# SyncE in program order, rows behind the sixth weight piece, and table constants on GpSimd

## The chip, the cores and the metric

One core of a Trainium2 chip. The metric is the device time of one execution in microseconds (us), the median over several runs. An execution has five engines that matter here: TensorE (PE; its weight loads are PEld), VectorE (DVE), ScalarE (ACT), GpSimd (POOL) and SyncE (SP), which only loads registers and issues DMAs.

## The reference

Clustered attention (2 batches, 8 heads, 768 positions, head size 64; a query sees the keys of its own cluster), then a dense layer on 1536 tokens, then a layer of 8 experts of which each token takes two. The last layer is what the change touches:

```python
def _moe2_ref(x, w_gate, w_noise, noise, w1, w2):
    logits = x @ w_gate
    noisy_logits = logits + np.log1p(np.exp(x @ w_noise)) * noise
    top2 = np.argpartition(-noisy_logits, 2, axis=1)[:, :2]
    ...
    for e in range(E):                      # E = 8, D = 512, F = 1024
        for k in range(2):
            mask = top2[:, k] == e
            h = np.maximum(x[mask] @ w1[e], 0.0)
            out[mask] += top2_w[mask, k, None] * (h @ w2[e])
```

## The kernel before, in words

**Stages.** Attention, the dense layer for batch 0 and for batch 1, a stage called `middle`, and the expert layer `moe2`; `rest` is a loop for overflowing tokens, which runs zero times on this input. Every token's row (512 numbers and 4 of routing) is scattered by POOL, by indirect DMA (`route_scatter`, L1043), into a DRAM table `xs` with a region for each expert. An expert reads its rows from there.

**Experts.** Experts 0 and 1 run in two halves of 240 rows, one per batch. The first halves, of batch 0, are computed in `middle` and at the start of `moe2`; meanwhile batch 1 is routed and scattered (six blocks, two scatters each). `gather_half(1)` (L1166, tile `Xh`) loads batch 1's rows of both experts; it has to wait for all of batch 1's scatters. Experts 2 to 7 are taken in an order found on the device (`ord`, `ordi`, ranked by their loads), with room for 432, 416, 408, 400, 392 and 384 rows.

**An expert's weights** come in eight pieces of 512 KB, in the order 0, 4, 1, 5, 2, 6, 3, 7 (`ORDER`): pieces 0 to 3 are columns of w1 (L1117), 4 to 7 rows of w2 (L1119). A piece lands in one of three staging buffers (`stg`); ACT rounds each half of it (L1126, "split" below) and DVE or POOL takes the remainder (L1130). Two sets of weight tiles (`wA` with `wg`, `wB` with `wx`) alternate between experts, so a piece's tiles come free when the expert before last has read them. An expert's rows (L1158, tile `X`) go into one buffer, which comes free when PE has transposed the rows before (L1229).

**In an expert** (`expert`, L1380 on) PE goes through eight blocks `fb`: first product (L1325), then ACT makes `hh` (L1333) and DVE `hl` (L1334), then the second product (L1348, or L1378 for experts 2 to 6). Results are weighted into `Y` by DVE (L1362) and scattered to the output by POOL (L1363); for all but a token's first expert `Y` starts from the rows gathered out of the output (L1210).

**What sets the order.** Each engine runs its instructions in one fixed order. Inside `manual_schedule(engines=...)` the named engines keep the order in which the program emits them; everything else, and where an ordered engine's instructions fall among those emitted outside, is placed by a planner from its own estimate of times. In attention all engines are ordered by hand, in `middle` all but POOL (table `WIN`); in `moe2` none is (but PE in the last expert's tail), SP included. `moe2` emits, on SP: `gather_half(1)`; then for each expert 2 to 7 a register load of its number (L1433), its eight pieces, its rows (`load`, L1432). An expert's `load` is emitted one turn ahead of its work.

**The rounds' table.** `route_end` (called near the end of `middle`, due time `re`) runs on DVE: it clips the counts, ranks the experts (`rank`) and writes the table for `rest` (`table`, L1083 on), with constants that don't depend on data: memsets of `caps`, `cap`, `tb`, `mx`, and columns made of `ie`. One of the six routing copies that precede the scatters (L1041) comes behind it in DVE's order. `consts` (L622) makes other constants at step 1 of attention.

Of the kernel before, what the change touches and what calls it, by code (L numbers as in the profile page):

```python
# [613 lines left out]
class Moe:  # L614
# [38 lines left out]

    def init_piece(self, i):
# [395 lines left out]
    def route_end(self):  # L1050
        v, end = self.nc.vector, self.rtot[:, NB, 0:2]
# [3 lines left out]
        self.rank(self.rtot[:, NB, :])  # L1055
        self.table(self.rtot[:, NB, :])

    def rank(self, total):

        c, v, n = self.const, self.nc.vector, E - 2  # L1060
        key, pos = c.tile([128, n], F32, name="key"), c.tile([128, n], F32, name="rpl")
        big = self.rtile("big", n, n)
        self.ord, self.cap = c.tile([128, n], F32, name="ord"), c.tile([128, E], F32, name="cap")
        self.ordi = c.tile([128, n], I32, name="ordi")
        v.scalar_tensor_tensor(key, total[:, 2:], float(E), self.ie[:, 2:], op0=OP.mult, op1=OP.subtract)
        row = lambda a: a[:, None, :].to_broadcast([128, n, n])
        col = lambda a: a.rearrange("p (n o) -> p n o", o=1).to_broadcast([128, n, n])
        v.tensor_tensor(big, row(key), col(key), op=OP.is_gt)
        v.tensor_reduce(pos.rearrange("p (n o) -> p n o", o=1), big, axis=AX.X, op=OP.add)
        v.tensor_tensor(big, row(pos), col(self.ie[:, :n]), op=OP.is_equal)  # L1070
        at = self.rtile("at", n, n)
        v.tensor_tensor(at, big, row(self.ie[:, 2:]), op=OP.mult)
        v.tensor_reduce(self.ord.rearrange("p (n o) -> p n o", o=1), at, axis=AX.X, op=OP.add)
        v.tensor_copy(self.ordi, self.ord)
        caps = c.tile([128, n], F32, name="caps")
        for r, (cp, ck) in enumerate(CAPS):
            v.memset(caps[:, r:r + 1], float(cp * ck))
        v.tensor_tensor(at, big, col(caps), op=OP.mult)
        v.memset(self.cap[:, :2], float(CAP))
        v.tensor_reduce(self.cap[:, 2:].rearrange("p (n o) -> p n o", o=1), at.rearrange("p r n -> p n r"),  # L1080
                        axis=AX.X, op=OP.add)

    def table(self, total):  # L1083
        nc, v = self.nc, self.nc.vector
        tb = self.const.tile([128, ROUNDS, E, 4], F32, name="tb")
        v.memset(tb, 0.0)
        for r in range(1, ROUNDS):
            o = BASE + CMIN + (r - 1) * CAP
            v.tensor_scalar_add(tb[:, r, :, 0], total, float(-o))
            v.tensor_scalar(tb[:, r, :, 1], self.ie, float(REG), float(o), op0=OP.mult, op1=OP.add)  # L1090
            v.tensor_copy(tb[:, r, :, 2], self.ie)
        v.tensor_scalar_add(tb[:, 1, :, 3], self.cap, float(-CMIN))
        nc.sync.dma_start(self.tab.rearrange("(o r) n -> o (r n)", o=1), tb[0:1].rearrange("p r e n -> p (r e n)"))
        mx = self.const.tile([128, 1 + ROUNDS], F32, name="mx")
        left = self.const.tile([128, E], F32, name="left")
# [3 lines left out]
        v.memset(mx[:, 1:2], 1.0)  # L1099
        for r in range(1, ROUNDS):  # L1100
# [469 lines left out]
```

## Time and profile before

| | us |
|---|---|
| median of 3 runs | 939.82 (936.96 to 941.28) |
| the profiled execution, its own time | 941.51 |
| its span, first to last instruction | 939.6 |

The span is what the rows below are read from; the 1.9 us around it are start and end. Times in rows are us from the span's start. A timeline row gives start, length, engine, line, operation, written tile and read tiles, how many were merged, and in square brackets the idle time before it and what ended it. SPq and POOLq are the queues of instructions that issue or wait.

### The profile page before, as it was taken

To read this page: it belongs to the slowest core of one execution; us is meant where nothing else is said; L and a number is where in the kernel's file an instruction comes from. 1 tells how busy PE (TensorE), PEld (TensorE's weight loads), DVE (VectorE), ACT (ScalarE), POOL (GpSimd) and SP (SyncE) were. 2 spreads that over 40 slices of the span, in tenths; PEclk is the share of its full clock that TensorE was granted. 3 is DMA by queue.
4 is the path that set the end of the run, shared out by engine and by line. 5 is a ranking of instruction groups with operands and counts; after the bars stand their busy time and mean duration, and the time that the engine had idled before them with its cause. 6 is when DMAs were issued, how large, how long until landed. Compare 5 with 4: busy or idle time off the path is not lost. (4 is left out here: it accounts for less than half of the span.)

```text
span 939.6 us, 14934 instructions
## 1 busy us (share of the span) xinstructions
PE 887.8 (94%) x5277; PEld 812.0 (86%) x5277; DVE 592.7 (63%) x1190; ACT 489.6 (52%) x1021; POOL 374.8 (40%) x398
## 2 busy tenths in 40 slices
PE   6999999999898999999999999899999899999993
PEld 4898989899887888888998979888889799999992
DVE  3889898998884667675447643836564445555231
ACT  2788888888794556554445433414444243432210
POOL 3134443454455988880000601562341334342121
PEclk8999999999898999999999999899999899999997
DMA  8756675677331344311111331274774737552120
GB/s 212 192 145 184 165 202 137 177 186 206 110 127 33 111 135 119 118 42 61 44 28 32 144 88 46 90 243 121 242 208 117 182 109 210 171 178 68 33 66 35
DMA packets 77532, 120.14 MB, mean 128 GB/s; under 512 B 9858, under 2 KB 55939, under 8 KB 76941
## 3 DMA queue, kind: packets, MB, share of 16 engines
q1 hardware_dynamic: 69997, 100.98, 37.5%
q0 software_dynamic: 7456, 18.16, 6.1%
q8 instruction: 43, 0.70, 0.3%
q14 instruction: 36, 0.29, 0.1%
HBM read 72.85 MB, written 23.76 MB: 103 GB/s over the span
## 5 line engine op out<-in xcount | busy, mean ns | idle before, releaser
L434 DVE TENSOR_TENSOR PTl<-ps_pt,PTh 128x384 fp32r<-128x384 f32 x192 | 98.8, 549 | 11.5 <-ACT PTh L429 10.4
L429 ACT ACTIVATE PTh<-ps_pt 128x384 fp32r<-128x384 f32 x192 | 87.9, 497 | 29.1 <-PE ps_pt L419 28.0
L402 DVE TENSOR_REDUCE nm<-ps_s 128x1 f32<-128x768 f32 x96 | 91.2, 950 | 15.1 <-PE ps_s L397 14.8
L419 PE MATMUL ps_pt<-ident,P 128*128 128x128 f32 x576 | 88.2, 277 | 3.8 <-DVE PTl L434 3.5
L410 ACT ACTIVATE P<-ps_s,nm 128x768 f32<-128x768 f32 x96 | 87.3, 910 | 4.9 <-DVE nm L402 4.9
L1333 ACT ACTIVATE hh<-bank 128x240 fp32r<-128x240 f32 (+6 forms) x80 | 35.2, 446 | 90.7 <-PE bank L1325 84.7
L1325 PE MATMUL bank<-xT,wB 128*128 128x240 f32 (+3 forms) x480 | 82.1, 319 | 0.0
L419 PEld LDWEIGHTS ps_pt<-ident,P 128*128 128x128 f32 x576 | 68.4, 141 | 13.8 <-DVE PTl L434 10.8
L1325 PEld LDWEIGHTS bank<-xT,wB 128*128 128x128 f32 x480 | 76.7, 189 | 2.5 <-DVE hl L1334 0.3
L1130 POOL TENSOR_TENSOR wA<-stg,wA 128x512 fp32r<-128x512 f32 x16 | 20.7, 1296 | 139.1 <-DVE wol L714 66.7
L822 PE MATMUL bank<-woh,gh 128*128 128x512 f32 x192 | 76.2, 397 | 0.0
L822 PE MATMUL bank<-wol,gh 128*128 128x512 f32 x192 | 75.0, 391 | 0.0
L1334 DVE SCALAR_TENSOR_TENSOR hl<-bank,hh 128x240 fp32r<-128x240 f32 (+6 forms) x80 | 40.2, 505 | 49.0 <-ACT hh L1333 48.2
L396 PE MATMUL ps_s<-k,q 128*128 128x384 f32 x192 | 70.7, 368 | 0.4 <-ACT P L410 0.2
L822 PE MATMUL bank<-woh,gl 128*128 128x512 f32 x192 | 70.7, 391 | 0.0
L397 PE MATMUL ps_s<-k,q 80*128 80x384 f32 x192 | 66.3, 346 | 2.6 <-DMA q<-ohT 2.6
L1363 POOL DMA_INDIRECT out_dram<-Y,idx x31 | 33.2, 1071 | 77.3 <-DVE Y L1362 68.5
L1126 ACT ACTIVATE wA<-stg 128x512 fp32r<-128x512 f32 x52 | 32.5, 632 | 43.5 <-DMA stg<-in_moe_w_dram 15.6
L454 PE MATMUL ps_o<-PTl,vs 128*128 128x256 f32 x288 | 54.0, 296 | 0.0
L454 PE MATMUL ps_o<-PTh,vs 128*128 128x256 f32 x288 | 53.7, 295 | 0.3 <-ACT T L461 0.2
L1325 PE MATMUL bank<-xT,wA 128*128 128x240 f32 (+3 forms) x300 | 53.2, 328 | 0.0
L1325 PEld LDWEIGHTS bank<-xT,wA 128*128 128x128 f32 x300 | 49.6, 197 | 1.3
(311 smaller groups left out, 2322.6 us busy)
## 6 DMA issues: line engine op xcount, KB each, us to landing
stg<-in_moe_w_dram SPq DMA_DIRECT2D x64, 512.0 KB
q<-ABq SPq DMA_DIRECT2D x48, 192.0 KB
k<-ABk SPq DMA_DIRECT2D x48, 192.0 KB
si<-in_moe_w_in_dram SPq DMA_DIRECT2D x14, 512.0 KB
so<-in_moe_w_out_dram SPq DMA_DIRECT2D x14, 512.0 KB
xs<-zrow SPq DMA_DIRECT2D x24, 217.7 KB
ld<-in_k_dram SPq DMA_DIRECT2D x8, 384.0 KB
ld<-in_q_dram SPq DMA_DIRECT2D x8, 384.0 KB
```

What stands on the lines that cost most here:

```text
L396: self.nc.tensor.matmul(o, self.g("S1", u, "q")[:, h, qs], self.g("S1", u, "k")[:, h, ks], start=True, stop=False)
L397: self.nc.tensor.matmul(o, self.g("S2", u, "q")[:80, h, qs], self.g("S2", u, "k")[:80, h, ks], start=False, stop=True)
L402: self.nc.vector.tensor_reduce(nm, self.g("s", j)[:, :, :384], axis=AX.XY, op=OP.max, negate=True)
L410: self.nc.scalar.activation(P, self.t.pop(("s", j))[:, :, :384], AF.Exp, bias=self.t.pop(("nm", j)), scale=1.0, accum_out=self.g("sums", u ...
L419: self.nc.tensor.transpose(ps[:, k, :], P[:, k * 128:(k + 1) * 128], self.ident)
L429: self.nc.scalar.activation(self.pt_at(j, g, 0), self.g("pt", j, g), AF.Copy)
L434: self.nc.vector.tensor_sub(self.pt_at(j, g, 1), self.t.pop(("pt", j, g)), f(self.pt_at(j, g, 0)))
L454: self.nc.tensor.matmul(self.g("O", u, qp)[:, h, :], vs[:, h, 2 * i + half].rearrange("p a d -> p (a d)"), PTx[:, kc, :], start=(c == 1 an ...
L822: nc.tensor.matmul(acc[j], g[:, sl], w, start=(fb == 0 and n == 0), stop=(fb == FB1 - 1 and n == 2))
L1325: self.nc.tensor.matmul(ps, w[:, kb, :], xT[:, kb, x], start=(kb == 0 and i == 0), stop=(kb == KB - 1 and i == 2))
L1333: self.nc.scalar.activation(hh, ps, AF.Relu)
L1334: self.nc.vector.scalar_tensor_tensor(hl, ps, 0.0, f(hh), op0=OP.max, op1=OP.subtract)
```

## The change

SP is ordered by hand in `moe2` too. `load` issues an expert's rows behind its sixth weight piece instead of behind the eighth. In `route_end`, `rank` and `table` are merged; the clipping of the first two counts comes after the ranking; the parts that don't depend on data are made by POOL in `consts`; three instructions over a row each become one over three rows; the unused first row of the table is dropped. On DVE `route_end` has 18 instructions instead of 37; on POOL `consts` has 18 more.

```diff
     def consts(self):
...
+        g, n, r = nc.gpsimd, E - 2, ROUNDS - 1
+        self.caps, self.cap = c.tile([128, n], F32, name="caps"), c.tile([128, E], F32, name="cap")
+        for i, (cp, ck) in enumerate(CAPS):
+            g.memset(self.caps[:, i:i + 1], float(cp * ck))
+        g.memset(self.cap[:, :2], float(CAP))
+        self.tb, self.offs = c.tile([128, r, E, 4], F32, name="tb"), c.tile([128, r, E], F32, name="offs")
+        g.memset(self.tb, 0.0)
+        for i in range(r):
+            o = BASE + CMIN + i * CAP
+            g.memset(self.offs[:, i], float(o))
+            g.tensor_scalar(self.tb[:, i, :, 1], self.ie, float(REG), float(o), op0=OP.mult, op1=OP.add)
+            g.tensor_copy(self.tb[:, i, :, 2], self.ie)
+        self.mx = c.tile([128, 1 + ROUNDS], F32, name="mx")
+        g.memset(self.mx[:, 1:2], 1.0)
...
     def route_end(self):
...
+        v.tensor_tensor(self.tb[:, :, :, 0], total[:, None, :].to_broadcast([128, ROUNDS - 1, E]), self.offs,
+                        op=OP.subtract)
+        v.tensor_scalar_add(self.tb[:, 0, :, 3], self.cap, float(-CMIN))
...
+        v.tensor_tensor(mx[:, 2:], mx[:, 0:1].to_broadcast([128, ROUNDS - 1]), self.offs[:, :, 0], op=OP.is_gt)
...
-    def weights(self, e, par):
+    def weights(self, e, par, late=lambda: None):
         we = [w[bass.ds(e, 1)].rearrange("o k n -> (o k) n") for w in (self.w1, self.w2)]
         W = [None] * 8
-        for s in ORDER:
+        for n, s in enumerate(ORDER):
             W[s] = self.weights_part(e, par, s, we)
+            if n == 5:
+                late()
         return [x for p in W for x in p]
...
         def load(e):
             i = self.nc.values_load(self.ordi[0:1, e - 2:e - 1], engines=(mybir.EngineType.SP,), min_val=2, max_val=E - 1)
-            n["W"] = self.weights(i, e % 2)
-            n["X"] = self.gather(i, *CAPS[e - 2])
+            n["W"] = self.weights(i, e % 2, lambda: n.__setitem__("X", self.gather(i, *CAPS[e - 2])))
...
-    moe.moe2(s["W"], W1, *s["A"][1][1:])
+    with tc.manual_schedule(engines={mybir.EngineType.SP}):
+        moe.moe2(s["W"], W1, *s["A"][1][1:])
     moe.rest()
```

## Rows read from the trace of the kernel before

**Rows 1.** The page, busy time of each engine.

```profile
PE 887.8 (94%) x5277; PEld 812.0 (86%) x5277; DVE 592.7 (63%) x1190; ACT 489.6 (52%) x1021; POOL 374.8 (40%) x398
```

**Rows 2.** Timeline of PE, in the expert layer; brackets: idle before.

```profile
635.34 0.66 PE L1229 MATMUL bank<-ident,Xh 120*128 120x120 f32 x2 [2.88 <-DMA Xh<-xs]
...
642.85 1.19 PE L1348 MATMUL bank<-wA,hh 128*120 128x512 f32 x4
...
676.23 0.44 PE L1229 MATMUL bank<-ident,X 108*128 108x108 f32 x3
...
692.76 0.55 PE L1229 MATMUL bank<-ident,X 104*128 104x104 f32 x4 [0.90 <-DMA X<-xs]
...
742.14 3.14 PE L1378 MATMUL bank<-hh,wB 128*128 128x416 f32 x8 [3.92 <-ACT hh L1333]
```

**Rows 3.** Stretches: length, busy PE, PEld, DVE, ACT, POOL, PEclk, DMA share, GB/s.

```profile
635.10:638.50 3.40, 3.16 (x10) 2.54 (x11) 1.86 (x9) 0.74 (x2) 1.07 (x1) 0.50 0.76 189
...
740.90:747.80 6.90, 5.66 (x17) 5.30 (x18) 5.61 (x12) 3.48 (x7) 2.46 (x2) 0.51 0.48 160
```

**Rows 4.** Timeline of SP, 600 to 632 us.

```profile
615.19 0.40 SPq L1117 DMA_DIRECT2D stg<-in_moe_w_dram  x1
...
631.03 0.81 SPq L1166 DMA_DIRECT2D Xh<-xs  x2
```

**Rows 5.** Timeline of POOL, 620 to 636 us.

```profile
621.35 1.29 POOL L1130 TENSOR_TENSOR wB<-stg,wB 128x512 fp32r<-128x512 f32 x1
...
625.32 0.97 POOL L1043 DMA_INDIRECT xs<-R,rridx  x1 [0.30 <-issue]
...
635.12 1.07 POOL L1210 DMA_INDIRECT Y<-out_dram,idx  x1 [0.30 <-issue]
```

**Rows 6.** Line L1043 (batch 1's 12 scatters): issue to landing.

```profile
DMA to landing us min/median/max: 3.0/3.9/6.2
```

**Rows 7.** Waits of SP, 590 to 660 us: us in total, times, longest.

```profile
SPq L1166 <- DMA out_dram<-Y,idx: 5.8, 1, 5.8
```

**Rows 8.** Timeline of DVE: expert 1's first half put into Y.

```profile
639.08 1.41 DVE L1362 SCALAR_TENSOR_TENSOR Y<-bank,m,Y 120x512 f32<-120x512 f32 x2 [1.41 <-PE bank L1348]
```

**Rows 9.** Timeline of SP around the rows of experts 3 and 4.

```profile
684.60 0.34 SPq L1158 DMA_DIRECT2D X<-xs  x1
...
713.47 0.62 SPq L1119 DMA_DIRECT2D stg<-in_moe_w_dram  x1
727.04 0.29 SPq L1158 DMA_DIRECT2D X<-xs  x1
727.59 0.37 SPq L1117 DMA_DIRECT2D stg<-in_moe_w_dram  x1
```

**Rows 10.** Waits of SP, whole span: us in total, times, longest.

```profile
SPq L1158 <- PE bank L1229: 30.1, 3, 12.8
```

**Rows 11.** Timeline of ACT behind the rows of experts 4 and 5.

```profile
732.05 0.52 ACT L1333 ACTIVATE hh<-bank 128x416 fp32r<-128x416 f32 x1 [3.83 <-PE bank L1325]
740.53 1.15 ACT L1126 ACTIVATE wB<-stg 128x512 fp32r<-128x512 f32 x2 [7.96 <-DMA stg<-in_moe_w_dram]
...
778.22 0.51 ACT L1333 ACTIVATE hh<-bank 128x408 fp32r<-128x408 f32 x1 [2.78 <-PE bank L1325]
782.06 1.15 ACT L1126 ACTIVATE wg<-stg 128x512 fp32r<-128x512 f32 x2 [3.33 <-DMA stg<-in_moe_w_dram]
```

**Rows 12.** Timeline of DVE in `route_end`: first constants, and the copy behind it.

```profile
613.80 0.10 DVE L1077 MEMSET caps<- 128x1 f32 x6
...
614.73 0.25 DVE L1091 COPY tb<-ie 128x8 f32<-128x8 f32 x1
...
616.50 0.16 DVE L1041 COPY R<-rmeta 128x4 f32<-128x4 f32 x1
```

**Rows 13.** Timeline of POOL in attention: the last constant and what follows it.

```profile
14.03 0.13 POOL L637 IOTA re<- 128x8 f32 x1
41.22 1.01 POOL L341 TENSOR_TENSOR sc<-eq,rev 128x384 f32<-128x384 f32 x1 [27.06 <-DVE eq L335]
```

More of the change, by code (lines that the diff above doesn't have):

```diff
@@ L1050, in route_end @@
     def route_end(self):
-        v, end = self.nc.vector, self.rtot[:, NB, 0:2]
+        nc, c, v, n = self.nc, self.const, self.nc.vector, E - 2
+        total, end = self.rtot[:, NB, :], self.rtot[:, NB, 0:2]
+        row = lambda a: a[:, None, :].to_broadcast([128, n, n])
+        col = lambda a: a.rearrange("p (n o) -> p n o", o=1).to_broadcast([128, n, n])
+        key, pos = self.rtile("key", n), self.rtile("rpl", n)
+        big, at = self.rtile("big", n, n), self.rtile("at", n, n)
+        self.ord, self.ordi = c.tile([128, n], F32, name="ord"), c.tile([128, n], I32, name="ordi")
+        v.scalar_tensor_tensor(key, total[:, 2:], float(E), self.ie[:, 2:], op0=OP.mult, op1=OP.subtract)
+        v.tensor_tensor(big, row(key), col(key), op=OP.is_gt)
+        v.tensor_reduce(pos.rearrange("p (n o) -> p n o", o=1), big, axis=AX.X, op=OP.add)
+        v.tensor_tensor(big, row(pos), col(self.ie[:, :n]), op=OP.is_equal)
+        v.tensor_tensor(at, big, row(self.ie[:, 2:]), op=OP.mult)
+        v.tensor_reduce(self.ord.rearrange("p (n o) -> p n o", o=1), at, axis=AX.X, op=OP.add)
+        v.tensor_copy(self.ordi, self.ord)
+        v.tensor_tensor(at, big, col(self.caps), op=OP.mult)
+        v.tensor_reduce(self.cap[:, 2:].rearrange("p (n o) -> p n o", o=1), at.rearrange("p r n -> p n r"),
+                        axis=AX.X, op=OP.add)
         over = self.rtile("over", 2)
@@ L1054, in route_end @@
         v.scalar_tensor_tensor(end, over, float(MAIN), self.over[:, 0], op0=OP.add, op1=OP.add)
[L1055 to L1095, printed above, removed]
+        v.tensor_tensor(self.tb[:, :, :, 0], total[:, None, :].to_broadcast([128, ROUNDS - 1, E]), self.offs,
+                        op=OP.subtract)
@@ L1096, in table @@
+        v.tensor_scalar_add(self.tb[:, 0, :, 3], self.cap, float(-CMIN))
+        nc.sync.dma_start(self.tab.rearrange("(o r) n -> o (r n)", o=1),
+                          self.tb[0:1].rearrange("p r e n -> p (r e n)"))
+        left, mx = self.rtile("left", E), self.mx
         v.scalar_tensor_tensor(left, self.cap, float(BASE), total, op0=OP.add, op1=OP.is_lt)
@@ L1098, in table @@
         v.tensor_reduce(mx[:, 0:1], left, axis=AX.X, op=OP.max)
-        v.memset(mx[:, 1:2], 1.0)
-        for r in range(1, ROUNDS):
-            v.tensor_single_scalar(mx[:, r + 1:r + 2], mx[:, 0:1], float(BASE + CMIN + (r - 1) * CAP), op=OP.is_gt)
+        v.tensor_tensor(mx[:, 2:], mx[:, 0:1].to_broadcast([128, ROUNDS - 1]), self.offs[:, :, 0], op=OP.is_gt)
         self.nr = self.const.tile([128, 1], I32, name="nr")
@@ L1187, in gather_rest @@
         t = self.cs.tile([CP, 4], F32, tag="t", name="t")
-        nc.sync.dma_start(t, self.tab[bass.ds(r * E + e, 1)].to_broadcast([CP, 4]))
+        nc.sync.dma_start(t, self.tab[bass.ds((r - 1) * E + e, 1)].to_broadcast([CP, 4]))
         sl = self.cs.tile([CP, CK, 4], F32, tag="sl", name="sl")
@@ L1473 @@
     xs = dram.tile([E * REG, ROW], F32, name="xs")
-    tab = dram.tile([ROUNDS * E, 4], F32, name="tab")
+    tab = dram.tile([(ROUNDS - 1) * E, 4], F32, name="tab")
     ident = const.tile([128, 128], F32, name="ident")
```

## The prediction

> **What bounds the kernel now.** I read the page's busy times first. TensorE is busy 887.8 us, 94% of the span of 939.6 us [rows 1], so 51.8 us are all that can be won without taking work from it, and an edit counts only where PE stands still or runs at its low clock. The next view is PE's timeline through the expert layer, where three pauses fall in the part that the change reorders [rows 2]: 2.88 us at 632.5, until the second half's rows of experts 0 and 1 (`Xh`) have landed; 0.90 us at 691.9, until expert 3's rows (`X`) have landed; 3.92 us at 738.2, until ScalarE has made an `hh`. Behind the first and the third the stretches show a granted clock of 0.50 for 3.4 us and 0.51 for 6.9 us, which is the 1.2 GHz level instead of 2.4 [rows 3]. PE was busy 3.16 and 5.66 us there, so at the full level it would have needed about half: 1.6 and 2.8 us more are lost to the clock. The three pauses are thus worth 4.5, 0.9 and 6.7 us. The constants and the route's end run on VectorE and GpSimd, and neither appears in these three brackets.
>
> **Part 1: SP in the program's order.** In the trace of before SP issues three weight pieces of expert 2, the first at 615.19, and only then `Xh` at 631.03 [rows 4]. In program order `Xh` comes first. It can't leave before batch 1's scatters have landed. POOL issues the last at 625.32 [rows 5]; the twelve take 3.0 to 6.2 us to land, median 3.9 [rows 6]. The 5.8 us wait ahead of `Xh` is put down to an output scatter [rows 7], but the first of the last pair (1.3 us ahead of 625.32), at the maximum of 6.2, lands at 630.2 too, and the 6.2 fall where two of the three pieces move. Without these pieces I take 3.3, between the least and the median: 625.3 + 3.3 = 628.6, so `Xh` leaves 2.4 us earlier. From issue to PE's use it took 635.34 − 631.03 = 4.3 us; then PE would wait 0.45 instead of 2.88 us. So short a wait should spare the low clock, 1.6 us. That makes −4.0. What is late next: the second product of expert 0's second half (642.85 now, [rows 2]) needs the two banks which DVE empties into `Y` at 639.08 and, merged in one row, about 0.7 us later [rows 8]; that in turn needs output rows whose gather POOL issues at 635.12 [rows 5]. Emptied at 640.5 at the latest, the banks allow 2.4 us; with the gathers about 1 us earlier, as the scatters ahead of them lose the same traffic, 3.4. I take **−3.4**, bounds −4.5 (pause and clock gone) and 0 (the last scatter lands at its 6.2 whatever else moves). The three pieces leave some 15 us later, right behind `Xh`. Their tiles are free only when expert 0 has read them, from about 642 on, and at 4.3 us behind `Xh` they are there by then: 0. If that cover were gone, the splits of ACT ahead of the next `hh` would be late by what is missing.
>
> What waits in SP's order: `Xh` now stands ahead of everything of expert 2, including the register load of its number, and the six loads of numbers stay each with its expert. A load of a register is under 1 us and each comes before a transfer that waits for a buffer anyway: 0.
>
> **Part 2: rows behind the sixth piece.** Expert 3's rows leave SP at 684.60, right behind the last piece [rows 9], though their buffer is free when PE has transposed expert 2's rows, at 676.7 [rows 2]. Two pieces earlier they leave by 677, land some 7 us earlier, and the pause at 691.9 goes: **−0.9**, bounds −0.9 and 0. For expert 2 the same is worth nothing, as PE has no pause at its transposes.
>
> From expert 4 on it is otherwise. SP reaches the rows at 714.1 and can't issue them until 727.04 [rows 9]: the buffer is held by expert 3's transposes. Three such waits sum to 30.1 us, the longest 12.8 [rows 10]. The rows leave at the same moment after the change, but the two pieces behind them, 3 and 7, now wait as well: SP reaches the rows already behind the sixth piece, so that some 7 to 12 us more of SP's time are a wait, and the experts' last two pieces leave behind the rows instead of ahead of them. Behind expert 4's rows today follow three pieces of expert 5; then it will be two of expert 4 and one of expert 5. As many bytes leave at the same moment. None of these pieces is due soon: expert 4's first `hh`, at 778.22, comes 51 us after its rows have left [rows 9, 11]. So the moved issues (two pieces and one transfer of rows, six times) cost PE nothing by themselves. What decides is where the planner puts their splits in ACT's order. Today one such split stalls ACT for 7.96 us at 732.6, because the first piece behind the rows takes from 727.59 to 740.53, and the `hh` behind it makes PE's pause of 3.92 [rows 9, 11]. I take this pause as staying: **0**, bounds −6.7 (pause and clock gone) and +17.0 (below).
>
> The Trainium skill ("DMA: Bandwidth & Descriptors", section "Why a DMA increments its semaphore by 16 and not by 1") says that a transfer from SP's queue runs on the largest number of DMA engines up to 16 that divides its rows: 102 partitions (expert 4) get six, 128 sixteen. By it the transfer of 102 rows is the slowest and holds up most what follows on its engines; the 12.9 us of the piece behind it agree.
>
> **Part 3: the route's end on DVE.** 19 of 37 instructions go. Six memsets take 0.10 merged, three table columns 0.25 [rows 12]; at 0.06 to 0.08 us each the 19 are 1.1 to 1.5 us, and the routing copy behind them at 616.50 comes that much earlier. The scatter that reads it starts only at 624.0, after ten others and two tensor operations on POOL, the first at 621.35 [rows 5, 12], so the gain lies beside POOL's work: **0**. Bounds: 0 and −2.6, if the planner, with the copy ready sooner, puts the last two scatters ahead of those two operations; that gain is inside the −4.5 above. The moved clipping has the same cost in a new place.
>
> **Part 4: 18 instructions on POOL in attention.** They follow the last constant at 14.03; then POOL idles 27.06 us [rows 13]. The nearest row, the 128x8 iota, takes 0.13, so they need 2.4 us: hidden eleven times over. The price can only be DVE, held up while POOL works on the same memory: at most the 2.4 us, at least 0. I take **+0.2**, near the small end, since the operands are 8 to 96 numbers a row.
>
> **Sum.** −3.4 − 0.9 + 0 + 0 + 0.2 = −4.1 against the profiled execution's 941.51 (span 939.6 and 1.9 around it): 937.4. That execution lies 1.7 us above the median of 939.82, so on the median's scale **935.7**. About 0.5%, 4.7 us, is what a measurement of this kernel can tell from no change, so this forecast lies just inside the band.
>
> **The rivals.**
>
> *A, the pause at 738 goes too.* SP's forced order changes the planner's times, and with other pieces behind expert 4's rows ACT's order there is made anew. If `hh` comes ahead of the late split, 3.92 + 2.8 us are saved: 935.7 − 6.7 = 929.0. For it: PE needs `hh` at 738 and ACT is idle from 732.6. Against it: the planner put a split there once, and the same bytes are as late.
>
> *B, the late splits come ahead of the first `hh` (slower).* The tiles of an expert's pieces 3 and 7 are free when the rows leave, while those of the next expert's first pieces come free only when its first product is read. So the planner may set pieces 3 and 7 earlier in ACT's order than today's splits. Behind expert 4's rows the first `hh`, at 732.05 now, would wait for the landing at 740.53 and two halves of 0.6: PE pauses 9.1 instead of 3.9 us, +5.2. Behind expert 5's the `hh` at 778.22 would wait for the piece that was there at 782.06: to 783.2, +5.0. For experts 6 and 7 no row shows the case; I take half, 2.6 each. With 1.6 of low clock: +17.0, so 953. It is slower than before as soon as a quarter of it (4.2 us) comes true, that is, one expert's rows; half of it gives 944. Against it: ACT waited 3.33 us for a piece behind expert 5's rows without any pause of PE [rows 11].
>
> By the rule of the Trainium skill in “DMA: Bandwidth & Descriptors” named above, the harm would be largest behind expert 4's rows and least behind expert 7's; it would shift B's prices between the experts, not their start.
>
> *C, `Xh` leaves no earlier.* If its release is the output scatter that the row names (issued behind the last scatter of rows), or the scatters land as late without the pieces, only 0.9 is won: 939.82 − 0.7 = 939.1.
>
> **How the numbers follow.** Forecast (sum holds, pause at 738 stays, between 933 and 938): 0.37. A: 0.25. B: 0.21. C: 0.17. Faster by over 0.5% (below 935.1): all of A and about half of the forecast, as its bounds (−4.5, 0 for `Xh`) lie on both sides: 0.44. Slower (above 944.5): most of B: 0.18. Within: 0.38. The range takes in the forecast, C, A with 2 us more, and B to its half: 927 to 947.
>
> **What would show it.** SP's timeline: `Xh` ahead of all pieces of expert 2, at about 628.6; the landing of the last scatters near 3.3 us. PE's timeline: no `Xh` pause over 1 us and clock 1.00 behind it; no pause on `X`. POOL: a block of 18 instructions at 14 to 17 us with an idle stretch of over 20 us behind it. ACT's timeline at the rows of experts 4 to 7: which comes first, a split waiting for `stg` or `hh`. I am wrong if `Xh` still leaves after 630.5, or if PE's waits for `hh` in the expert layer, 3.92 us in the largest now, sum to over 10 us.

## The result, and the profile after

The changed kernel takes **949.41 us** (median of 16 runs, 940.67 to 955.60) against 939.52 for the kernel before (16 runs, 936.61 to 941.61): a ratio of **1.0099, 95% interval 1.0080 to 1.0118**. It is slower by 1%, where 935.7 was forecast, and lies above the range. Two of the changed kernel's runs, 955.29 and 955.60, count as slow and are not in the ratio. Its profiled execution took 949.89 us, span 948.1.

The page's busy times of the kernel after show no more work on PE than [rows 1]:

```profile
PE 885.6 (93%) x5277; PEld 808.1 (85%) x5277; DVE 596.2 (63%) x1171; ACT 490.1 (52%) x1021; POOL 377.4 (40%) x416
```

So PE stands still more. Timeline of PE after, the four longest pauses of the expert layer (compare [rows 2]):

```profile
629.94 0.63 PE L1226 MATMUL bank<-ident,Xh 120*128 120x120 f32 x4 [1.67 <-DMA Xh<-xs]
...
686.54 1.02 PE L1226 MATMUL bank<-ident,X 104*128 104x104 f32 x5 [4.80 <-DMA X<-xs]
...
745.57 1.75 PE L1375 MATMUL bank<-hh,wB 128*128 128x416 f32 x4 [4.41 <-ACT hh L1330]
...
802.98 1.39 PE L1375 MATMUL bank<-hl,wA 128*128 128x408 f32 x3 [2.68 <-DVE hl L1331]
```

The pause on `Xh` shrank from 2.88 to 1.67 us. The one on expert 3's rows, which was to vanish, grew from 0.90 to 4.80; the one for `hh` stayed, and one for `hl` is new. Stretches of both kernels, before first: from PE's first transposes of `Xh` to expert 2's first product, then the stages of experts 2, 3 and 4, each from its first product to the next (columns as in [rows 3]):

```profile
635.34:685.59 50.25, 50.04 (x322) 43.77 (x323) 31.58 (x72) 24.47 (x55) 15.16 (x13) 0.97 0.58 180
685.59:727.26 41.67, 40.77 (x215) 38.40 (x214) 21.73 (x36) 17.71 (x35) 13.43 (x11) 1.00 0.57 164
727.26:773.50 46.24, 42.32 (x225) 41.08 (x224) 20.25 (x36) 14.45 (x30) 14.18 (x12) 0.93 0.54 145
773.50:813.33 39.83, 39.08 (x225) 38.31 (x225) 21.00 (x39) 16.40 (x32) 14.54 (x12) 1.00 0.57 168
```

and after, with two rows more for the stretches behind the pauses at 686.54 and 745.57 (granted clock 0.53 and 0.51, the 1.2 GHz level):

```profile
629.94:690.31 60.37, 52.50 (x336) 45.34 (x336) 32.89 (x76) 26.05 (x57) 18.64 (x15) 0.97 0.65 198
690.31:730.11 39.80, 39.80 (x207) 37.84 (x206) 19.87 (x32) 14.88 (x29) 10.86 (x9) 1.00 0.41 111
730.11:777.18 47.07, 42.66 (x226) 41.36 (x224) 22.04 (x37) 15.02 (x31) 14.31 (x12) 0.93 0.53 143
777.18:821.54 44.36, 40.79 (x226) 39.83 (x224) 23.16 (x38) 15.72 (x31) 14.55 (x12) 0.96 0.51 150
686.40:690.00 3.60, 3.46 (x13) 2.92 (x14) 1.10 (x2) 1.41 (x3) 1.27 (x1) 0.53 0.32 115
744.80:751.70 6.90, 6.13 (x18) 5.88 (x19) 6.15 (x8) 4.06 (x8) 5.38 (x5) 0.51 0.54 166
```

I call the first two stretches together **S1** (from `Xh` to expert 3) and the other two **S2** (experts 3 and 4). S1 went from 91.9 to 100.2 us, S2 from 86.1 to 91.4. Behind S2 nothing changed (813.33 to PE's last matmul at 924.29 before, 821.54 to 932.65 after: 111.0 and 111.1).

These 13.6 us are more than the 8.5 between the spans, because S1 also starts 5.4 us earlier. Only a part of that is the change's. Timeline of PE before, at the last matmuls of the routing (`rrM`) and at a first product of the second halves, 244 matmuls later in both orders:

```profile
600.97 0.22 PE L993 MATMUL bank<-rrM,tri 128*128 128x48 bf16 x1 [2.38 <-DVE rrM L943]
...
644.56 1.51 PE L1325 MATMUL bank<-xT,wg 128*128 128x240 f32 x12
```

and after, with a later pause in between:

```profile
597.80 0.20 PE L1008 MATMUL bank<-rrM,tri 128*128 128x48 bf16 x1 [2.37 <-DVE rrM L958]
...
638.55 0.71 PE L1322 MATMUL bank<-xT,wg 128*128 128x240 f32 x4 [1.02 <-DVE xT L1229]
...
641.19 1.50 PE L1322 MATMUL bank<-xT,wg 128*128 128x240 f32 x12
```

At `rrM` this execution stood 3.2 us ahead of the one before; a second profile of the same changed program (after_2 below) stood 2.0 us behind it (602.99). So this lead can't be put down to the change. Counted from `rrM`, the first product shown comes after 43.6 us before and 43.4 after: the gain at `Xh` is down to 0.2 us there, as PE pauses for an `xT` (the transposed rows, whose remainder DVE takes). DVE was late with it because the instruction ahead of it stood 1.52 us for output rows. Timeline of DVE after:

```profile
637.43 0.75 DVE L1359 SCALAR_TENSOR_TENSOR Y<-bank,m,Y 120x512 f32<-120x512 f32 x1 [1.52 <-DMA Y<-out_dram,idx]
638.10 0.40 DVE L1229 TENSOR_TENSOR xT<-bank,xT 128x240 fp32r<-128x240 f32 x1
```

Expert 3's first product comes 126.3 us after `rrM` before and 132.3 after (128.3 in after_2). On this count the change loses 6.0 us up to expert 3 (2.0 in after_2) and 5.3 in S2 (4.4).

Timeline of SP after: `Xh`, expert 3's rows, expert 4's rows and the pieces behind them (compare [rows 4, 9]):

```profile
625.15 0.81 SPq L1163 DMA_DIRECT2D Xh<-xs  x2
...
674.47 0.37 SPq L1155 DMA_DIRECT2D X<-xs  x1
678.15 0.38 SPq L1112 DMA_DIRECT2D stg<-in_moe_w_dram  x1
...
710.35 0.37 SPq L1114 DMA_DIRECT2D stg<-in_moe_w_dram  x1
729.89 0.33 SPq L1155 DMA_DIRECT2D X<-xs  x1
730.47 0.38 SPq L1112 DMA_DIRECT2D stg<-in_moe_w_dram  x1
```

`Xh` leaves 5.9 us earlier, but 3.1 of these are the lead of this execution: its last scatter was issued at 622.22, the one before at 625.32. From that scatter to `Xh` it is 2.9 us instead of 5.7, and to expert 3's rows 52.3 instead of 59.3. SP stands in front of expert 4's rows for 19.2 us, where the longest such wait was 12.8 [rows 10], and pieces 3 and 7 stand behind them. Timeline of ACT after, at the piece behind expert 3's rows and the one behind expert 4's (compare [rows 11]):

```profile
687.45 1.15 ACT L1121 ACTIVATE wB<-stg 128x512 fp32r<-128x512 f32 x2 [6.25 <-DMA stg<-in_moe_w_dram]
688.51 0.35 ACT L1330 ACTIVATE hh<-bank 128x240 fp32r<-128x240 f32 x1
...
743.97 1.15 ACT L1121 ACTIVATE wA<-stg 128x512 fp32r<-128x512 f32 x2 [8.50 <-DMA stg<-in_moe_w_dram]
745.02 0.50 ACT L1330 ACTIVATE hh<-bank 128x416 fp32r<-128x416 f32 x1
```

Each time ACT waits for a piece that left right behind the rows (9.3 us from issue to split in the first case, 13.5 in the second), and an `hh` stands behind the split.

The constants cost what was forecast. Timeline of POOL after in attention: first and last of the 18 instructions, then 24.80 us of idle time (compare [rows 13]):

```profile
14.34 0.26 POOL L657 MEMSET caps<- 128x1 f32 x6
...
16.33 0.10 POOL L667 MEMSET mx<- 128x1 f32 x1
41.22 1.01 POOL L341 TENSOR_TENSOR sc<-eq,rev 128x384 f32<-128x384 f32 x1 [24.80 <-DVE eq L335]
```

**The programs' own orders** differ in one way that no view of before shows. In the order of PE's instructions as built, expert 3's first transposes stand 30 matmuls behind expert 2's first product in the kernel before, and 14 ahead of it in the changed one; expert 2's stand 130 ahead of it before, 188 ahead after. On ACT, at the start of expert 3's stage (x: `xT`, y: `yT`, H: `hh`, wA, wB: splits):

```
before:  x x wA wA y y x x wA  H  wB wB  H  wB wB  H
after:   x x wA y y x x        H  wA wA  H  wA wA wB wB wB  H
```

The planner made these orders anew. The two wA pairs of the line of after are pieces 3 and 7 of expert 4, which are not used for another 30 us.

### The profile page after: what moved, and what is told of

It is laid out like the page before. It is cut to its first block, busy times and chain, and to the rows that moved or that the text cites. A ratio compares the mean times of both kernels' runs of the same rounds, so it can differ in the third digit from the quotient of the medians.

```text
span 948.1 us, 14924 instructions
## 1 busy us (share of the span) xinstructions
PE 885.6 (93%) x5277; PEld 808.1 (85%) x5277; DVE 596.2 (63%) x1171; ACT 490.1 (52%) x1021; POOL 377.4 (40%) x416
## 5 line engine op out<-in xcount | busy, mean ns | idle before, releaser
L1331 DVE SCALAR_TENSOR_TENSOR hl<-bank,hh 128x240 fp32r<-128x240 f32 (+6 forms) x80 | 40.2, 505 | 59.4 <-ACT hh L1330 58.9
```

Source lines behind the costliest of these rows:

```text
L1331: self.nc.vector.scalar_tensor_tensor(hl, ps, 0.0, f(hh), op0=OP.max, op1=OP.subtract)
```

## The experiments

Ratios are to the kernel before on the same chip. One thing has to be known to read them: on four of the five chips whose number is on record ACT stands 8 to 10 us at an `hh` near 620, whatever the kernel. Timeline of ACT of the kernel before on such a chip (before_2):

```profile
621.67 0.63 ACT L1333 ACTIVATE hh<-bank 128x240 fp32r<-128x240 f32 x2 [10.22 <-remote]
```

and of PE there:

```profile
622.09 1.21 PE L1348 MATMUL bank<-wB,hh 128*120 128x512 f32 x2 [5.60 <-ACT hh L1333]
```

The trace names no releaser. PE is late from there on, finds `Xh` landed, and the kernel before takes some 4 us more (medians 943.3 to 944.8 on these chips; 939.3 on the fifth chip and 939.5 in the first measurement, whose chip is not on record). The change as a whole was timed only without this wait, so ratios with and without a star are not compared closely.

| run | what it is | S1, us | S2, us | profile less median, us | ratio (95%) |
|---|---|---|---|---|---|
| before | first profile | 91.9 | 86.1 | +2.0 | |
| before_2 * | second profile, ACT's wait | 91.9 | 88.4 | +3.1 | |
| after | the change | 100.2 | 91.4 | +0.5 | 1.0099 (1.0080–1.0118) |
| after_2 | the change again | 96.2 | 90.5 | +2.7 | 1.0093 (1.0064–1.0122) |
| late_only * | rows alone | 94.8 | 88.2 | −0.8 | 1.0067 (1.0044–1.0091) |
| no_late * | all but the rows | 92.3 | 86.5 | −0.7 | 0.9997 (0.9980–1.0015) |
| manual_only * | SP's order alone | 93.9 | 86.5 | +1.3 | 1.0013 (0.9983–1.0043) |
| late2 * | expert 2's rows only | 96.3 | 84.9 | +0.9 | 1.0025 (0.9996–1.0054) |
| late3 * | expert 3's rows only | 97.5 | 88.0 | +3.4 | 1.0061 (1.0037–1.0085) |
| late4on * | rows of 4 to 7 only | 93.3 | 94.6 | +2.7 | 1.0065 (1.0040–1.0089) |
| late4s * | late4on, ACT held | 91.4 | 84.8 | −1.2 | 1.0005 (0.9974–1.0035) |
| fix_x | the change, PE held | 98.1 | 90.6 | +2.7 | 1.0099 (1.0067–1.0131) |
| fix_s | the change, ACT held, 4 on | 103.9 | 83.6 | +1.7 | 1.0067 (1.0042–1.0091) |
| fix_xs | both | 100.1 | 85.9 | −2.4 | 1.0109 (1.0072–1.0145) |
| fix_s3 * | ACT held, 3 on | 104.6 | 85.4 | +8.0 | 1.0047 (1.0026–1.0067) |
| fix_xs3 * | and PE held | 91.9 | 85.4 | −5.1 | 1.0037 (1.0016–1.0059) |
| fix_x2s3 * | and expert 2's transposes | 94.2 | 85.0 | +3.2 | 1.0033 (1.0006–1.0061) |
| hold3 * | no_late, ACT held | 91.5 | 83.9 | −3.8 | 0.9994 (0.9972–1.0016) |
| hold5 * | at one place | 91.8 | 82.8 | −3.0 | 0.9989 (0.9965–1.0013) |
| hold5b * | fewer splits | 92.1 | 86.1 | +0.2 | 1.0023 (0.9992–1.0054) |

\* chips with ACT's wait. S1 and S2 are read from the stretches of one profiled execution each, by the same marks as above; the last column but one tells how far that execution lies from its kernel's median (before_2: from the median of the kernel before on its chip). The ratio is over all timed runs. In before, before_2 and late_only the transposes of `Xh` stand five matmuls later in PE's order than in the others, which makes their S1 about 1 us shorter.

S1 is a rough measure where rows are moved: after, after_2 and fix_s have the same order on PE and on ACT up to 744 us, and S1 is 100.2, 96.2 and 103.9.

### Which part carries the loss

late_only is the kernel before with this edit (and `load` passing the rows' `gather` as `late`); no_late is the changed kernel with 7 in place of 5:

```diff
-        for s in ORDER:
+        for n, s in enumerate(ORDER):
             W[s] = self.weights_part(e, par, s, we)
+            if n == 5:
+                late()
```

> The kernel before with one part of the change alone: an expert's rows are issued behind its sixth weight piece. Theory 1 (new plan): moving the rows is what makes the planner re-order PE and ACT. In this kernel's program PE meets expert 3's transposes ahead of expert 2's first product, as in the changed kernel (there 4.80 us of pause on the rows' DMA), and ACT has the late pieces' splits in the changed kernel's places. So nearly the whole loss is here: 945 to 951 us, ratio 1.006 to 1.012 of before, with a pause of 3 to 5 us on X ahead of expert 2's first product and one of 3 us or more for hh near expert 4's rows. Theory 2 (SP's forced order): SP's own order decides, through Xh and expert 2's pieces; then this kernel is within 0.3% of before. Theory 3 (constants on GpSimd and the short route end): also within 0.3% of before.

> The changed kernel with the rows put back behind the eighth piece: SP's order by hand and the constants stay. Theory 1: the loss is gone and what is left is the gain at Xh, 1.2 to 3 us: 936 to 939 us, ratio 0.996 to 1.000 of before; Xh leaves ahead of expert 2's pieces, PE's pause on it is under 2 us. Theory 2: still slow, 944 to 950 us, expert 2's stage long. Theory 3: still slow, 944 to 950 us.

Both came out by theory 1: the rows alone carry the loss (ratio 1.0067), without them it is gone (0.9997). Two sizes were off: late_only's pauses on `X` are 2.05 (expert 2) and 1.83 us (expert 3) instead of 3 to 5, and no_late shows no gain at `Xh`. The orders in the traces say the same: no_late and the kernel before differ on PE only around the transposes of `Xh`, and not on ACT; so do late_only and the changed kernel.

Then the rows expert by expert: the place became an argument of `weights`, passed by `load` as `5 if e == 3 else 7` (late3), `7 if e <= 3 else 5` (late4on) and `5 if e == 2 else 7` (late2):

```diff
-    def weights(self, e, par, late=lambda: None):
+    def weights(self, e, par, late=lambda: None, at=5):
...
-            if n == 5:
+            if n == at:
```

> The changed kernel with only expert 3's rows behind the sixth piece, all others behind the eighth. In this program PE has expert 3's transposes ahead of expert 2's first product, as in the changed kernel. Theory 1: the pause there comes back (4.8 us and about 1.7 of low clock, less the 0.9 of before), so about 5 us over the kernel with all rows behind the eighth piece: 941 to 944 us. Rival (the pieces behind expert 4's rows carry the loss): as the kernel with all rows behind the eighth piece, within 1.5 us of it.

> The changed kernel with only the rows of experts 4 to 7 behind the sixth piece; PE has expert 3's transposes at the places of before, and ACT has the splits of the late pieces of experts 4 on in nearly the changed kernel's places. Theory 1 with both halves: the late pieces cost 2 to 6 us by splits that stand ahead of hh, so 939 to 943 us and pauses of PE for hh or hl of over 2 us near 740 and 800. Rival (expert 3's hoisted transposes carry it all): within 1.5 us of the kernel with all rows behind the eighth piece.

> The changed kernel with only expert 2's rows behind the sixth piece, all others behind the eighth. PE has expert 2's transposes some 50 matmuls earlier than in the kernel before, and the rest as before. Theory 5 (a block of transposes that the planner moved ahead of rows still under way makes PE pause on X, and the low clock follows): pause on X of 1 to 5 us near 662, the stretch from Xh to expert 2's first product 52 to 60 us instead of 50; ratio 1.001 to 1.006, spread wider than that of before. Rival 5 (expert 2's rows do no harm, only those of expert 3 and on): ratio 0.998 to 1.001, stretch 49 to 52.

Each has its own pause. Timeline of PE, late3:

```profile
693.33 1.10 PE L1226 MATMUL bank<-ident,X 104*128 104x104 f32 x5 [4.33 <-DMA X<-xs]
```

late2:

```profile
663.55 1.22 PE L1226 MATMUL bank<-ident,X 108*128 108x108 f32 x7 [4.53 <-DMA X<-xs]
```

late4on:

```profile
744.93 2.45 PE L1375 MATMUL bank<-hh,wB 128*128 128x416 f32 x6 [7.74 <-ACT hh L1330]
```

late3 lengthens S1 by 5.2 us against no_late and S2 by 1.5; late4on lengthens S2 by 8.1 and S1 by 1.0. Their medians are 5.9 and 7.2 us above no_late's, late4on's more than the 2 to 6 expected. So there are two losses in two places, each of some 6 to 7 us; they don't add up in late_only (6.7), and no run tells why. late2's 1.0025 has 1 in its interval; its profile shows the pause that was expected (S1 96.3).

### Is it the order of PE and ACT, or the transfers?

`issue_after(ins)` orders a block's instructions behind `ins` on that engine, without a wait. SP's order stays the changed kernel's in all of these. fix_x holds expert 3's transposes (`pe_ins` is the last matmul of a first product):

```diff
+            with self.tc.issue_after(self.pe_ins) if e == 3 else ExitStack():
-            self.xpose(n["X"], n["xT"], (6, 7))
+                self.xpose(n["X"], n["xT"], (6, 7))
```

fix_s holds splits on ACT (`later` for experts 4 on, `first` for 5 on; `finish` is called by `expert` behind block 2, where `hh_ins` is its fourth `hh` and becomes `mid_ins`); fix_xs has both:

```diff
+            st = self.weights_load(s, we)
+            if n < 6 or not later:
+                with self.tc.issue_after(self.mid_ins) if n == 0 and first else ExitStack():
+                    split(s, st)
+            else:
+                rest.append((s, st))
...
+        def finish():
+            with self.tc.issue_after(self.hh_ins):
+                for x in rest:
+                    split(*x)
```

> The changed kernel once more, on the chip of the three runs beside it, as their base. Theory 1: ratio 1.006 to 1.012 of before, a pause of 3 to 5 us on X ahead of expert 2's first product, and a pause of 3 us or more for hh right behind expert 4's rows. Nothing else is expected of it; if those two pauses are absent while the ratio stays, theory 1 falls.

> The changed kernel, SP's order untouched, with one constraint on PE: the transposes of expert 3's rows may not stand ahead of the last block of expert 2's first product. Theory 1 (the planner moved the transposes ahead of rows that land 12 us after their issue): PE's pause of 4.80 us on X and the low clock behind it (1.7 us) go, the stretch from the first transposes of Xh to expert 2's first product falls from 60 to 50 to 54 us, and the whole is 5 to 8 us under the changed kernel. Rival (the earlier rows delay the weight pieces behind them, and that is the loss): ACT's wait for stg at the same place stays and PE then waits for hh; within 2 us of the changed kernel.

> The changed kernel, SP's order untouched, with one constraint on ACT: the splits of the two pieces behind the rows of experts 4 to 7, and of the next expert's first piece, may not stand ahead of the fourth hh of the expert in work. Theory 1 (ACT waits there for a piece that SP could not issue before the rows, and the hh behind it makes PE pause): the pauses of 4.41 and 2.68 us and their low clock go, the stages of experts 3 and 4 fall from 47.1 and 44.4 us to 40 to 42 each, 6 to 11 us under the changed kernel; the pause on X ahead of expert 2 stays at 3 to 5. Rival (the bytes themselves are too late, in whatever order ACT splits them): a pause of over 2 us stays in each of the two stages, for hh or for a weight tile; within 3 us of the changed kernel.

> Both constraints together. Theory 1: the two gains add up, 11 to 18 us under the changed kernel, ratio 0.990 to 0.999 of before, no pause of PE over 2 us between expert 2's and expert 5's first products. Rival (the loss is in the transfers, not in the order of PE and ACT): within 4 us of the changed kernel, slower than before.

after_2 repeats the result (1.0093), but its pause on expert 3's rows is 1.60 us, not 3 to 5. On this chip, then, fix_x had little to win there.

**fix_x fell out by the rival.** The pause on expert 3's rows is gone and nothing is won (median 948.70, after_2's 947.98). Timeline of SP of fix_x, at expert 3's rows:

```profile
680.22 0.37 SPq L1155 DMA_DIRECT2D X<-xs  x1
684.25 0.38 SPq L1112 DMA_DIRECT2D stg<-in_moe_w_dram  x1
```

of ACT, at the piece behind them:

```profile
692.87 1.15 ACT L1121 ACTIVATE wB<-stg 128x512 fp32r<-128x512 f32 x2 [6.62 <-DMA stg<-in_moe_w_dram]
693.92 0.77 ACT L1330 ACTIVATE hh<-bank 128x240 fp32r<-128x240 f32 x2
```

and of PE:

```profile
694.32 1.20 PE L1345 MATMUL bank<-wx,hh 128*120 128x512 f32 x4 [2.23 <-ACT hh L1330]
```

The piece behind the rows takes 8.6 us to its split, and the `hh` behind that split is PE's next pause: under the pause on `X` lay a second one. So theory 1 fell in its first form, that the transposes alone make S1's loss, as far as these two intervals of some 3 us to each side can tell.

**fix_s did in S2 nearly what theory 1 said**: 90.5 (after_2) to 83.6 us (stages of 43.4 and 40.2, where 40 to 42 were expected), the pauses of 4.41 and 2.68 us are gone, and what PE still waits in the stage of expert 3 is 2.6 us for two later `hh`. Timeline of ACT of fix_s in that stage; the splits stand behind the fourth `hh`, and their pieces have landed:

```profile
749.83 0.52 ACT L1348 ACTIVATE hh<-bank 128x416 fp32r<-128x416 f32 x1 [4.04 <-PE bank L1340]
750.25 1.14 ACT L1122 ACTIVATE wA<-stg 128x512 fp32r<-128x512 f32 x2
751.65 1.16 ACT L1122 ACTIVATE wA<-stg 128x512 fp32r<-128x512 f32 x2 [0.26 <-DMA stg<-in_moe_w_dram]
```

In total it won 2 us instead of 6 to 11 (1.0067, against 1.0093 with overlapping intervals), which is what its rival had for the time, though not for the pauses: expert 5's stage took 40.0 us instead of 38.4 (38.8 in after_2), and S1, where it changes no order, came out at 103.9. fix_xs shows no gain at all in its median, as its rival had it. On this chip, then, the holds moved the pauses, and the medians do not tell them from the change.

So the hold on ACT was taken to expert 3 (fix_s3: `later` for experts 3 on, with expert 3's splits behind expert 2's second `hh`; fix_xs3 with PE's hold as well), then to the transposes of expert 2 (fix_x2s3), and, the other way, to late4on alone (late4s):

```diff
+            with self.tc.issue_after(self.pe_ins if e == 3 else self.pe_mid) if e < 4 else ExitStack():
```

> The kernel with the constraint on ACT, extended by expert 3: the splits of its two pieces behind its rows may not stand ahead of the second hh of expert 2, those of the next expert's first piece not ahead of them either. Theory 4 (one mechanism for all experts: the piece right behind the rows lands 8 to 14 us after its issue instead of some 4, and what costs is that ACT's order has its split ahead of an hh that PE needs): ACT's wait of 6.2 to 6.6 us for stg between 685 and 693 goes. The stretch from Xh to expert 3's first product, 96 to 104 us in the kernels with the rows behind the sixth piece, falls to 92 to 97, and the whole to 939 to 944 us, ratio 1.000 to 1.005. Rival 4 (the rows of experts 2 and 3, 0.9 MB each, two pieces earlier in a stretch where the DMAs are busy 0.65 of the time, hold up everything behind them, whatever the order): the stretch stays at 96 us or more, ratio 1.005 to 1.011.

> The same with the constraint on PE as well (expert 3's transposes not ahead of the last block of expert 2's first product). Theory 4: neither a pause on X ahead of expert 2 nor one for hh behind it; 938 to 942 us, ratio 0.998 to 1.003. Rival 4: ratio 1.005 or more.

> All rows behind the sixth piece and SP's order as in the changed kernel; PE's transposes of expert 2 held to the places of before, those of expert 3 behind expert 2's last first product, and the splits of the pieces behind the rows held behind hh. Theory 5: no pause on X of over 1 us, the stretch from Xh to expert 2's first product 49 to 53 us, ratio 0.997 to 1.002. Rival 5 (the transfers themselves are the loss): stretch 54 us or more, ratio 1.003 to 1.008.

> The changed kernel with the rows of experts 2 and 3 behind the eighth piece again, those of experts 4 to 7 behind the sixth, and the constraint on ACT for the pieces behind these. Theory 5: with PE's transposes of experts 2 and 3 at the places of before and the splits behind hh, nothing of the loss is left: ratio 0.995 to 1.001, stretch from Xh to expert 2's first product 49 to 52 us, stages of experts 3 and 4 at 40 to 44 each. Rival 5 (pieces 3 and 7 behind the rows are too late in any order): ratio 1.003 or more.

**late4s settles experts 4 to 7**: with the same transfers in the same order on SP, 1.0065 becomes 1.0005 and S2 94.6 becomes 84.8. Its stages of experts 3 and 4:

```profile
726.44:768.07 41.63, 40.01 (x226) 38.78 (x224) 20.16 (x37) 14.69 (x30) 14.03 (x12) 1.00 0.61 161
768.07:811.28 43.21, 40.64 (x226) 39.88 (x225) 21.21 (x39) 15.75 (x32) 14.30 (x12) 0.96 0.57 154
```

The intervals do not meet (the two were measured on different chips, both with ACT's wait). The rival, that pieces 3 and 7 are too late in any order, falls: it is the engines' order that costs. Which engine's is shown less well. The edit holds splits on ACT alone, but the planner then ordered PE anew in S2 too; that ACT's split ahead of `hh` is the cause rests on the pause of 7.74 us in late4on, which is gone. The hold also removes the pause near 740 that the kernel before has itself; hold3 (below), the same kind of hold with all rows behind the eighth piece, came out at 0.9994, so the moved rows of experts 4 to 7 cost nothing that these runs can tell once the splits are held.

**Experts 2 and 3 are settled in part.** fix_s3's ratio came out as theory 4 had it, but its profile, which lies 8.0 us above its median, shows S1 at 104.6, with PE waiting 4.65 and 4.28 us on the rows of experts 2 and 3. fix_xs3 fell between theory 4 and its rival (1.0037); its profile, 5.1 us below its median, has no pause of over 1.2 us in S1 (91.9), so it shows only that an execution without the loss is possible with these transfers. With all holds (fix_x2s3) PE waits for no `X` any more and S1 is 94.2, but 1.0033 remains, which is what theory 5's rival had for the ratio, though S1's first stretch (53.1 us) is shorter than the rival's 54; it is half of late_only's 1.0067. Against late4s, on the same chip and with the same holds behind S2, it is 3.1 us more in the median and 2.8 in S1. Timeline of SP of fix_x2s3, at expert 2's rows and the piece behind them:

```profile
655.30 0.36 SPq L1173 DMA_DIRECT2D X<-xs  x1
660.10 0.38 SPq L1113 DMA_DIRECT2D stg<-in_moe_w_dram  x1
```

and ACT at the piece behind them, which no hold covers:

```profile
666.91 1.15 ACT L1122 ACTIVATE wA<-stg 128x512 fp32r<-128x512 f32 x2 [5.07 <-DMA stg<-in_moe_w_dram]
667.97 0.35 ACT L1348 ACTIVATE hh<-bank 128x240 fp32r<-128x240 f32 x1
```

It is the same pattern: PE pauses 1.69 us for that `hh`, 2.6 us for `hh` up to expert 3. Whether this is the rest, or the busier DMAs are (a share of 0.62 in S1's first stretch of fix_x2s3, 0.55 in late4s), stays open, as no run holds these splits.

### The gain at Xh

manual_only is the kernel before with `manual_schedule(engines={mybir.EngineType.SP})` around `moe2`, as the change has it; before_2 is the kernel before, unchanged.

> The kernel before with SP's order by hand alone. Prediction's part 1: Xh leaves 2 to 6 us earlier, and where PE's pause on Xh is the one that counts, 1 to 3.4 us are gained: ratio 0.996 to 0.999. Rival: where ACT's long wait near 615 holds PE up before Xh is wanted, Xh is there anyway and nothing is gained: ratio 0.999 to 1.001.

> The kernel before once more, for a second profile on this chip. Every theory: the pause for hh of 3 to 5 us near 740, the one for Xh of 2 to 4 us near 633, the stretch from Xh to expert 3's first product 91 to 93 us.

The rival holds here: SP issues `Xh` 2.8 us behind the last scatter in manual_only, 6.2 in before_2, and PE takes it without a pause in both, as it comes late from ACT's wait. That pause, expected in before_2 at 2 to 4 us, did not come, and its pause near 740 was 6.12 us, over the 3 to 5 expected; S1 (91.9) was as expected. No timed run tried this edit alone where PE does wait for `Xh`; there the profiles speak (a pause of 2.88 us before; 1.67 and 1.82 in the two of the change, with no low clock behind it, but a pause for `xT` of 1.02 and 1.34 soon after).

### Does a version beat both?

The kernel before has the same pattern: three pieces of expert 5 behind expert 4's rows, split ahead of an `hh`. hold3 is no_late with ACT held there and for experts 6 and 7, hold5 there only, hold5b with two pieces behind the third `hh` instead of three behind the fourth:

```diff
+            with self.tc.issue_after(self.mid_ins) if n < hold else ExitStack():
-            W[s] = self.weights_part(e, par, s, we)
+                W[s] = self.weights_part(e, par, s, we)
```

> The changed kernel with the rows behind the eighth piece again, and one constraint on ACT: the splits of the three pieces that follow the rows of experts 4 to 6 (pieces 0, 4 and 1 of the next expert) may not stand ahead of the fourth hh of the expert in work. Theory 4: before's own pause of 3.92 us for hh near 740 is the same mechanism, so it and its low clock (2.8 us) go: the stage of expert 3 falls from 46.2 to 40 to 43 us, and the whole to 932 to 937 us, ratio 0.992 to 0.998 of before: faster than both kernels. Rival 4: the pause stays above 2 us or turns into one for a weight tile; ratio 0.998 to 1.003.

> The changed kernel with the rows behind the eighth piece and the constraint on ACT at one place alone: the splits of the three pieces that follow expert 4's rows (pieces 0, 4 and 1 of expert 5) not ahead of the fourth hh of expert 3; nothing is held for experts 6 and 7. Theory: the stage of expert 3 falls from 46 to 41 to 43 us and those of experts 4 and 5 stay at 39.5 to 41 and 38 to 38.5, so 3 to 6 us are won: ratio 0.993 to 0.997 of before. Rival (a late piece is paid for somewhere, as the buffers it holds come free later): the stage of expert 4 or 5 grows by 2 us or more, ratio 0.998 to 1.002.

> The same place with fewer splits held: those of the two pieces right behind expert 4's rows, not ahead of the third hh of expert 3, which is about when they land. Theory: as hold5, and at least as good, as the buffers come free some 4 us earlier: ratio 0.993 to 0.997. Rival: a pause of 2 us or more stays at the third or fourth hh, ratio 0.998 to 1.002.

None can be told from the kernel before, about as the rivals had it. The pause near 740 goes in hold3 and hold5 (in hold5b one of 3.77 us stays), but a part comes back where the buffers, held longer, let the next piece leave later. Timeline of ACT of hold5:

```profile
743.58 3.23 ACT L1121 ACTIVATE wB<-stg 128x512 fp32r<-128x512 f32 x6
747.69 0.52 ACT L1331 ACTIVATE hh<-bank 128x416 fp32r<-128x416 f32 x1 [0.89 <-PE bank L1323]
758.09 1.15 ACT L1121 ACTIVATE wB<-stg 128x512 fp32r<-128x512 f32 x2 [9.88 <-DMA stg<-in_moe_w_dram]
```

and of PE:

```profile
759.69 1.02 PE L1376 MATMUL bank<-hh,wx 128*128 128x416 f32 x4 [2.79 <-ACT hh L1331]
```

These profiles (spans 938.9 and 936.6) are the best and nearly the best of their kernels' executions, so their S2 shows more than the medians do (944.43 and 941.45). Where splits are held for all later experts, S2 also leaves out a price: expert 5's stage takes 39.4 to 40.1 us in hold3, late4s and all kernels with fix_s, fix_xs or s3 in the name, 38.1 to 38.8 in the others.

## Why the prediction was wrong

**Part 1 (−3.4): the issue moved as forecast, the gain did not last; the term was mis-sized.** `Xh` left 2.9 us behind the last scatter, where 3.3 was forecast and 5.7 measured before; batch 1's scatters landed in 2.7 to 3.3 us (3.0 to 6.2 in [rows 6]). The pause left was 1.67 us, not 0.45: the transposes stand five matmuls earlier in PE's new order, so PE reached them 1.1 us earlier, and the rows took 0.5 us longer from issue to use. The low clock was spared, as forecast. Then the next thing was late: the text let it be the banks that DVE empties into `Y`, with the gather of their output rows about 1 us earlier, and allowed 2.4 to 3.4 us. Against the last scatter that gather came later instead (11.6 us behind it, 9.8 before); DVE stood for it, and PE for the `xT` behind. 0.2 us of the gain was left 244 matmuls behind `rrM` in both profiles of the change. no_late (0.9997) and manual_only (1.0013) ran where ACT's wait covers it.

**Part 2, expert 3's rows (−0.9, "bounds −0.9 and 0"): this is the step that failed first.** "Two pieces earlier they leave by 677, land some 7 us earlier, and the pause at 691.9 goes." Against the last scatter they did leave 7.0 us earlier, but took 12.1 us from issue to use (8.2 before), so they landed only 3.1 earlier (5.3 in after_2). That would still have covered the 0.90 us. But the step kept PE's order as it was: the planner, told of an earlier issue, set the transposes 44 matmuls earlier, and PE stood 4.80 us. And it gave the weight piece behind the rows no price: where PE's order was held (fix_x), this piece's split was late and PE waited 2.23 us for the `hh` behind it, with nothing won. In late3, where only these rows are moved, the median is 5.9 us above no_late's. How the loss divides between the transposes, that piece and the busier DMAs stays open. A bound of 0 towards a loss had no row behind it; the text itself said that the planner orders all this anew, and used it only for rivals A and B.

**Part 2, experts 4 to 7 ("0 … What decides is where the planner puts their splits"): the wrong value was chosen.** S2 took 5.3 us more (4.4 in after_2), and late4on's median is 7.2 us above no_late's. What happened is rival B's mechanism: ACT's order has the splits of pieces 3 and 7 ahead of `hh`, and late4s shows that the same transfers cost nothing in another order. B's price behind expert 4's rows was 5.2 us more pause; it was 0.5 more in the changed kernel and 3.8 more in late4on (7.74). Expert 4's stage then lost another 2.68 us and its clock at an `hl`. B's half, 8.5 us, is near S2's 8.1 in late4on, though not in the places that B priced. It was given 0.21, and its upper half was left out of the range.

The rule of the Trainium skill quoted in the prediction (“DMA: Bandwidth & Descriptors”, "Why a DMA increments its semaphore by 16 and not by 1") ranks the rows of experts 4, 5 and 6 (102, 100, 98 partitions: six, ten, fourteen engines). The trace agrees: the piece behind them took 13.5, 8.4 and 6.6 us from issue to split in the changed kernel. Expert 3's 104 partitions (thirteen by the rule) do not fit, with 9.3 us (6.0 before).

**Parts 3 and 4** held: the 18 instructions took 2.1 us, hidden, and neither edit moves PE's or ACT's order (no_late, which has both edits, and manual_only, which has neither, have the same orders on PE and ACT).

**Rivals A and C** did not come by their mechanisms, though C's price for `Xh`, nothing, is close to the 0.2 us left. Of the prediction's alarms, waits for `hh` of over 10 us in sum did not ring (6.5 us in the changed kernel): it looked at one kind of wait, and the largest new one was on `X`. Two of the signs it named without an alarm did fail: `Xh`'s pause is over 1 us, and there is one on `X`.

## What to carry to other kernels

Where a planner orders the engines, an edit to one queue changes the orders of all of them: read the new order on every engine before giving a price of 0, and ask of each moved consumer whether its transfer has really landed by then, by the time from issue to use in the trace. What stands right behind a large transfer landed late here (6.6 to 13.5 us from issue to split, 3.4 at the least elsewhere); keep its consumer behind everything that is due sooner, or the wait moves from one engine to the next. A hold that removes one wait shows first whether another lay under it.

## What the runs showed of the hardware

- On four of five chips ACT stands 8.1 to 10.4 us at nearly the same `hh`, in all 14 profiles made there; PE pauses 3.5 to 5.8 us behind it, and the trace gives no releaser. None of the six other profiles, of the fifth chip and of the first measurement, has it. What it is stays open.
- With the same order on PE and ACT, S1 took 100.2, 96.2 and 103.9 us (after, after_2, fix_s), and the executions of the changed kernel that enter the ratio lie between 940.67 and 954.45, those of the kernel before between 936.61 and 941.61. That waits placed directly on transfers make the time uneven is my reading; no run separates it.
- The length of a pause alone did not tell whether TensorE's granted clock fell behind it: behind 2.79 us (hold5, 759.69) and 2.31 us (late_only, 803.99) it stayed at 1.00, behind 1.71 us (fix_x, 804.55) and 1.92 us (fix_s, 639.53) it was 0.50, the 1.2 GHz level, for some 3 us.
